# A planned attention and feed-forward kernel: a position table for the planner's rules, scaled down weights kept in memory, three more copy buffers

## The chip, the cores and the metric

The kernel runs on one core of a Trainium2 chip. The metric is device time in microseconds, as the median of several runs. Five engines work side by side, each through its own list of instructions: TensorE (PE, matrix products), VectorE (DVE), ScalarE (ACT), GpSimd (POOL) and SyncE (SP, which here only issues transfers).

## The reference

One transformer block over 2048 tokens of width 512, with 32 heads of 16, all in bf16. A condition vector c gives six vectors of shifts, scales and gates:

```
mod = silu(c) @ w_mod                     # sa, ca, ga, sb, cb, gb
h = layernorm(x) * (1 + ca) + sa
q, k, v = heads(h @ wqkv)                 # 32 heads of 16
o = softmax(q k^T / 4) v
x = x + ga * (o @ wo)
h = layernorm(x) * (1 + cb) + sb
x = x + gb * ((gelu(h @ w_gate) * (h @ w_up)) @ w_down)     # 512 -> 1792 -> 512
```

The score matrices have 32 x 2048 x 2048 elements, and each needs an exponential. That is what most of the time goes into.

## The kernel before

**Work.** The queries are cut into nine sets (`SETS`): seven of 256 tokens and two of 128. A unit is one set of queries with one group of four heads; the first two sets, and for the first heads the last two, are taken together. For each unit PE multiplies queries and keys 32 rows at a time into `ps_sc`, two halves of three banks of 512 columns (`qk`). An exponential turns a half into bf16 in `E`, and PE multiplies E with the values into `ps_pv` (`pv_mms`). At a unit's end (`unit_end`) DVE copies the sums to `osb`, a small transfer chain spreads the denominators, and DVE normalises into `onorm`.

**Two ways to an exponential.** One exponential instruction of ACT takes two or three banks. When it takes two, DVE turns the third into an exponential with integer arithmetic: a multiply and add on the scores gives the bits of a power of two (`bits` in `stream`, in the profile `dreg`, `kq`, `mreg<-ps_sc`). Four such banks make a quad, and each quad needs three shifted copies (`shift_task`, `128x2048 uint16`), which PE multiplies with scaled copies of the values (`vs`) to correct the error of the approximation. The quads' banks lie in buffers `kq`, the copies in buffers `sq`; `room` says which buffers a unit may take.

**Side work.** Everything else is put between the score products: projections, output projection (`side_wo`), second layernorm (`side_t2`) and the feed-forward layer (`side_ffn`), all through the bank `ps_mi`. The first six sets are the flow sets (`FLOW`): each set's feed-forward streams its gate, up and down weights from memory in pieces of 256 KB (`load`, `load_down`). Since the down weights are not scaled by gb, `down_fin` multiplies the sum by gb into `xw` and then adds it to the residual `xs`. For the last sets the weights stay (`weight_parts`), and `scale_down` multiplies the resident down weights by gb once on DVE.

**What sets the order.** The kernel's order is not written out by hand. `stream` runs a model of the engines while it records instructions: at each step it probes when an operation could start, and takes a score product, a value product, a piece of side work or a filler product. Its rules are constants: how far ahead a quad may be chosen (`AHEAD`, 96), how full DVE may be (700, 150), when a copy is urgent (`URGENT`, `LATE`), how much side work must be due (1536, one half of a piece), and `TUNE`, of which all sixteen rows are alike. What is recorded is a fixed list for each engine; at run time only semaphores hold an instruction back. Fillers are products whose result is not used; `short` asks for them when PE has worked too little in the last few microseconds.

**The head** (`prologue`) loads the first tokens and weights, computes the modulation columns (`mod_cols`) and the first layernorm, transposes and projects, with 512-column warm-up products (`warm_up`) between.

Instructions are recorded by helpers, so the profile's lines are those of the helpers: L328 matmul, L332 transpose, L341 activation, L345 tensor_tensor, L353 tensor_scalar, L358 scalar_tensor_tensor, L362 copy, L391 transfers.

## Time and profile before

| | |
|---|---|
| median of 3 runs | 818.45 us (818.15 to 819.36) |
| span of the profiled execution | 817.5 us |
| ACT busy | 783.2 us (96%) |
| PE busy | 750.5 us (92%) |
| DVE busy | 742.8 us (91%) |
| read from HBM, written | 50.04 MB, 2.35 MB |
| mean granted clock of TensorE | 1.00 |

The profiled execution is one run; what the profile tells of it is its span, from the first to the last instruction, 817.5 us. The timed runs are 0.65 to 1.9 us longer than that.

How to read the rows: a group has the line, the engine, the operation, what it writes and reads, the shape of both, how often it ran, its busy time together, the mean duration of one in ns, and how long its engine stood idle just before such instructions, with what ended most of that. Durations of neighbours on one engine overlap a little, so the distance from one start to the next is shorter than a duration. In the view by stretches each engine has its busy time in a stretch and, in brackets, its instructions.

### The profile page before, as it was taken

The numbers are of one execution on the slowest core, as the hardware profiler recorded it, in microseconds if no ns is written. First come the engines' busy times: TensorE is split into PE (matmuls) and PEld (weight loads), VectorE is DVE, ScalarE is ACT, GpSimd is POOL, SyncE is SP. The second block draws the span as 40 slices with busy tenths as digits, with TensorE's granted clock in tenths as the row PEclk, the third lists the DMA queues.
The fourth block names the chain that finished last, engine by engine and source line by source line (L and its number), as shares of the span: only waits on it lengthen the run. The fifth ranks groups of instructions, "written<-read, shape, count | busy, mean of one in ns | idle before, by whom it ended". The sixth has DMA issues, their size and how long they took to land.

```text
span 817.5 us, 37365 instructions
## 1 busy us (share of the span) xinstructions
PE 750.5 (92%) x17184; PEld 366.4 (45%) x17188; DVE 742.8 (91%) x1496; ACT 783.2 (96%) x746; POOL 4.6 (1%) x13
## 2 busy tenths in 40 slices
PE   7899999998999898989999899998998899888998
PEld 3333334343543454435443444444443444346567
DVE  6876898899999999999999999999999999989874
ACT  5999999999999999999999999999999999999962
POOL 2000000000000000000000000000000000000000
PEclk9999999999999999999999999999999999999999
DMA  9100000021530153104420442034233541200000
GB/s 292 63 6 20 10 9 10 10 71 40 168 112 16 52 155 93 35 21 134 122 63 16 136 121 61 16 105 133 63 106 88 165 126 36 67 10 10 19 13 14
DMA packets 94499, 57.38 MB, mean 70 GB/s; under 512 B 17029, under 2 KB 91910, under 8 KB 94342
## 3 DMA queue, kind: packets, MB, share of 16 engines
q1 hardware_dynamic: 93812, 54.47, 23.6%
q8 instruction: 134, 2.20, 1.2%
q10 hardware_dynamic: 530, 0.53, 0.2%
q14 instruction: 23, 0.19, 0.1%
HBM read 50.04 MB, written 2.35 MB: 64 GB/s over the span
## 4 chain that ended last, share of the span: by engine, by line
ACT 88%; PE 9%; DVE 1%; issue 0%; DMA 0%; SPq 0%; DVEq 0%
ACT E L341 85%; PE ps_sc L328 4%; PE ps_mi L328 3%; ACT wreg L341 3%; PE ps_pv L328 2%; DMA xs<-in_A_x_dram 0%; DVE osb L362 0%; DVE xs L345 0%; DVE dreg L353 0%; DVE st L381 0%; DVE wreg L353 0%; DVE nwt L345 0%; PE ps_sc L332 0%; DVE wreg L358 0%; DVE mreg L353 0%
## 5 line engine op out<-in xcount | busy, mean ns | idle before, releaser
L341 ACT ACTIVATE E<-ps_sc 128x1024 bf16<-128x1024 f32 (+2 forms) x700 | 758.7, 1319 | 19.1 <-PE ps_sc L328 19.0
L328 PE MATMUL ps_sc<-qT,kT 32*128 32x256 bf16 (+3 forms) x2048 | 202.2, 273 | 25.2 <-ACT E L341 21.1
L328 PE MATMUL ps_sc<-qo,kT 32*128 32x256 bf16 (+2 forms) x2048 | 202.2, 273 | 16.9 <-ACT E L341 15.5
L328 PE MATMUL ps_pv<-E,vaug 128*17 128x256 bf16 (+2 forms) x3204 | 154.1, 273 | 3.8 <-DVE osb L362 2.7
L353 DVE TENSOR_SCALAR dreg<-ps_sc 128x512 uint16<-128x512 f32 x200 | 135.5, 687 | 6.8 <-PE ps_sc L328 5.8
L328 PE MATMUL ps_mi<-wreg,mreg 128*32 128x256 bf16 x2816 | 116.6, 275 | 6.5 <-DVE wreg L362 3.4
L328 PEld LDWEIGHTS ps_sc<-qT,kT 32*128 32x128 bf16 (+1 forms) x2048 | 62.3, 92 | 117.3 <-ACT E L341 105.1
L328 PEld LDWEIGHTS ps_sc<-qo,kT 32*128 32x128 bf16 x2048 | 62.1, 92 | 105.6 <-ACT E L341 94.9
L328 PEld LDWEIGHTS ps_pv<-E,vaug 128*17 128x17 bf16 x3204 | 60.4, 89 | 59.6 <-issue 39.8
L328 PEld LDWEIGHTS ps_mi<-wreg,mreg 128*32 128x32 bf16 x2816 | 63.7, 96 | 42.8 <-issue 24.8
L328 PE MATMUL ps_pv<-mreg,vs 128*17 128x256 bf16 (+2 forms) x1840 | 80.9, 268 | 0.6 <-DVE mreg L353 0.3
L353 DVE TENSOR_SCALAR kq<-ps_sc 128x512 uint16<-128x512 f32 x104 | 70.9, 688 | 8.6 <-PE ps_sc L328 8.2
L353 DVE TENSOR_SCALAR mreg<-dreg 128x2048 uint16<-128x2048 uint16 x100 | 67.5, 682 | 2.2 <-PE ps_pv L328 2.2
L353 DVE TENSOR_SCALAR mreg<-ps_sc 128x512 uint16<-128x512 f32 x96 | 65.0, 688 | 4.5 <-PE ps_sc L328 4.3
L328 PEld LDWEIGHTS ps_pv<-mreg,vs 128*17 128x17 bf16 x1840 | 40.7, 91 | 15.1 <-issue 4.7
L353 DVE TENSOR_SCALAR mreg<-mreg 128x2048 uint16<-128x2048 uint16 x71 | 47.4, 686 | 0.0
L328 PE MATMUL ps_mi<-hreg,wreg 128*32 128x512 bf16 (+1 forms) x496 | 36.6, 376 | 0.4 <-DVE vaug L362 0.3
L362 DVE CAST wreg<-ps_mi 128x512 bf16<-128x512 f32 x49 | 33.6, 686 | 2.4 <-PE ps_mi L328 2.2
L345 DVE TENSOR_TENSOR wreg<-wreg 128x1024 bf16<-128x1024 bf16 (+1 forms) x56 | 34.5, 618 | 0.0
L353 DVE TENSOR_SCALAR sq<-dreg 128x2048 uint16<-128x2048 uint16 x49 | 33.7, 687 | 0.8 <-PE ps_pv L328 0.8
L358 DVE SCALAR_TENSOR_TENSOR wreg<-wreg,ps_mi 128x512 bf16<-128x512 bf16 x49 | 33.4, 682 | 1.0 <-ACT wreg L341 0.5
L353 DVE TENSOR_SCALAR mreg<-kq 128x2048 uint16<-128x2048 uint16 x48 | 32.5, 683 | 0.0
(193 smaller groups left out, 722.7 us busy)
## 6 DMA issues: line engine op xcount, KB each, us to landing
mreg<-in_B_w_up_dram SPq DMA_DIRECT2D x46, 256.0 KB, 3.2
mreg<-in_B_w_gate_dram SPq DMA_DIRECT2D x42, 256.0 KB, 3.3
dreg<-in_B_w_down_dram SPq DMA_DIRECT2D x18, 256.0 KB, 3.5
rb<-scr_rec SPq DMA_DIRECT2D x120, 32.0 KB, 2.0
mreg<-in_B_w_down_dram SPq DMA_DIRECT2D x12, 256.0 KB, 3.7
ereg<-in_B_w_down_dram SPq DMA_DIRECT2D x12, 256.0 KB, 3.8
mreg<-in_w_mod_dram SPq DMA_DIRECT2D x1, 2048.0 KB, 11.8
out_dram<-xs SPq DMA_DIRECT2D x15, 128.0 KB, 1.7
```

The costliest lines, as they stand in the source:

```text
L328: return self.rec("pe", lambda e: e.matmul(out, lhsT, rhs, start=start, stop=stop, tile_position=tp), [lhsT, rhs], [out], cost=(n, int(rhs ...
L341: return self.rec("act", lambda e: e.activation(out, in_, func, scale=scale, **kw), rd, wr, cost=self.cost("act", out, [in_], "act"))
L345: return self.rec(eng, lambda e: e.tensor_tensor(out, a, b, op), [a, b], [out], cost=self.cost(eng, out, [a, b], "tt"))
L353: return self.rec(eng, lambda e: e.tensor_scalar(out, a, s1, s2, **kw), rd, [out], cost=self.cost(eng, out, [a], "ts") + 60 * (len(rd) - 1 ...
L358: return self.rec("dve", lambda e: e.scalar_tensor_tensor(out, a, s, b, op0=op0, op1=op1), rd, [out], cost=self.cost("dve", out, [a, b], " ...
L362: return self.rec(eng, lambda e: e.tensor_copy(out, in_), [in_], [out], cost=self.cost(eng, out, [in_], "ts"))
```

## The change

1. The planner's constants become one row of fourteen numbers, and `TUNE` a table of 33 rows, one for each 64 positions of the score sequence (`rules`). In the order of a row: the ACT slack in which side work may start, the credit below which a quad may start in the later part, the number of waiting DVE steps, a DVE look-ahead, the two bounds on DVE's load, the old `LATE`, the old `URGENT`, how far ahead a quad may lie, the old `AHEAD`, the share of a piece that must be due, the credit at which side work goes first, the rate of credit in per cent, and DVE's lead in the background step.
2. The down weights are multiplied by gb in the first flow set, right after their load, and written to a new tensor `wd_scaled` in memory. All later loads read that tensor; `scale_down` and the second operation of `down_fin` go.
3. Three more buffers for shifted copies, in parts of `hreg`, `mreg` and `dreg` that are free in some stages; `room` opens them by stage. `ones` and `half`, which lay in that part of `dreg`, get tiles of their own. The loads of the last pieces of gate and down weights wait for the buffer in `hreg`.
4. In `prologue` six warm-up products go.
5. The model's least time of a product over the whole array is 158 columns instead of 64. This changes the planner's view only.

```diff
-AHEAD = (30, 44)
-URGENT = 9
-LATE = 2
-TUNE = ((600, 3500, 6, 120),) * 16
+STEP = 64
+RULES = (600, 3500, 6, 120, 700, 150, 2, 9, 96, 30, 2, 1536, 100, 150)
+TUNE = (
+    (1000, 4097, 6, 120, 700, 150, 2, 9, 96, 30, 2, 1536, 100, 150),
+    (600, 3500, 6, 120, 700, 150, 2, 3, 96, 30, 2, 1536, 100, 150),
+    (600, 3500, 6, 120, 700, 150, 2, 3, 96, 27, 3, 1536, 100, 0),
...
+)
-            end = t + max(cols + (12 if mode else 6), 64) / 2.4
+            end = t + max(cols + (12 if mode else 6), 64 if mode else 158) / 2.4
-        self.sq += [ereg[:, :], onorm[:, 2048:4096]]
+        self.sq += [ereg[:, :], onorm[:, 2048:4096], hreg[:, NFC * 256:NFC * 256 + 2048], mreg[:, 10240:12288], dreg[:, 10 * D:14 * D]]
-        self.ones = dreg[:, 10 * D:10 * D + P]
-        self.half = dreg[:, 10 * D + P:10 * D + 2 * P]
+        self.ones = sb("ones", [P, P], BF16)[:, :]
+        self.half = sb("half", [P, 2], BF16)[:, :]
+        self.wdg = self.dram("wd_scaled", [F, D], BF16).rearrange("(f p) n -> p f n", p=P)
-        self.warm_up(4)
+        self.warm_up(1)
         self.mod_cols(self.scp[:, 1, 0:8], 0, range(4))
-        self.warm_up(3)
-        dv = self.B_w_down.rearrange("(f p) n -> p f n", p=P)
+        dv = self.wdg
-        return ([piece(0, i, g[i]) for i in range(6)] + [piece(0, 6, g[6], [("ffn", 0)]), piece(2, 6, d[6], [("ffn", 0)])]
+        return ([piece(0, i, g[i]) for i in range(6)] + [piece(0, 6, g[6], [last, "sq"]), piece(2, 6, d[6], [last, "sq"])]
-    def scale_down(self):
...
-    def down_fin(self, bank, t, flow=False):
-        if flow:
-            self.tt("dve", self.xw, bank, self.gb[:, :], ALU.mult)
-        self.tt("dve", self.xs[:, t, :], self.xs[:, t, :], self.xw if flow else bank, ALU.add)
+    def down_fin(self, bank, t):
+        self.tt("dve", self.xs[:, t, :], self.xs[:, t, :], bank, ALU.add)
-                v = self.B_w_down.rearrange("(f p) n -> p f n", p=P)
-                self.task([("sp", lambda: self.dma("sp", self.wdst[i], v[:, 2 * i:2 * i + 2, :], "sd%d" % i))], ("wl", gi, 2, i))
+                v = self.wdg if gi else self.B_w_down.rearrange("(f p) n -> p f n", p=P)
+                steps = [("sp", lambda: self.dma("sp", self.wdst[i], v[:, 2 * i:2 * i + 2, :], "sd%d" % i))]
+                if not gi:
+                    steps += [lambda x=x: self.tt("dve", self.wdst[i][:, x, :], self.wdst[i][:, x, :], self.gb[:, :], ALU.mult) for x in range(2)]
+                    steps += [("sp", lambda: self.dma("sp", self.wdg[:, 2 * i:2 * i + 2, :], self.wdst[i], "ws%d" % i))]
+                self.task(steps, ("wl", gi, 2, i),
+                          (lambda: NSQ in self.sq_free) if i > 4 else (lambda: NSQ + 4 in self.sq_free) if i in (1, 2) else None)
-        return 0 if self.plain[tk[1][1]] * 512 <= URGENT * tk[1][1][3] else 2
+        return 0 if self.plain[tk[1][1]] * 512 <= self.tune[7] * tk[1][1][3] else 2
+    def rules(self, i):
+        self.tune = TUNE[min(i, len(TUNE) - 1)]
-                ok = range(NK if pool is self.quad_free else NSQ + (u in units[:4]))
+                ok = list(range(NSQ))
+                if ("ffn", FLOW - 1) in self.have:
+                    ok += [NSQ, NSQ + 3]
+                elif ("q", 3, NDC - 1) in self.have:
+                    ok += [NSQ + 2]
+                elif ("t2T", 0) not in self.have:
+                    ok += [NSQ, NSQ + 4]
-            self.tune = TUNE[min(pos // P, 15)]
+            if pos // STEP != stage:
+                stage = pos // STEP
+                self.rules(stage)
-                if len(mem) == CH and c > 2 and self.free["dve"] < max(t + 700, self.free["act"] + 150):
+                if len(mem) == CH and c > 2 and self.free["dve"] < max(t + self.tune[4], self.free["act"] + self.tune[5]):
-                    self.credit = min(self.credit + rate * len(items), 4096)
+                    self.credit = min(self.credit + rate * len(items) * self.tune[12] / 100, 4096)
```

The remaining lines of the diff put other numbers of the row in the place of the old constants in the same way.

## The prediction

> **What bounds the kernel now.** I read the page first (engines, chain), then busy time by stretch, then the groups of ScalarE and VectorE, last the timeline of the first 16 us.

> ```profile
> PE 750.5 (92%) x17184; PEld 366.4 (45%) x17188; DVE 742.8 (91%) x1496; ACT 783.2 (96%) x746; POOL 4.6 (1%) x13
> ...
> ACT 88%; PE 9%; DVE 1%; issue 0%; DMA 0%; SPq 0%; DVEq 0%
> ```

> ScalarE (ACT) is busy for 96% of the span, and 88% of the chain that ended last runs through it. VectorE (DVE) and TensorE (PE) come close, so the stretches must tell who waits. In the next view each row is a stretch, and each engine has its busy time in it.

> ```profile
> core 0: us, PE busy (x) PEld busy (x) DVE busy (x) ACT busy (x) POOL busy (x), PEclk, DMA share, GB/s
> 9.53:16.45 6.92, 4.89 (x72) 3.32 (x71) 3.84 (x12) 3.70 (x7) 0.00 (x0) 1.00 0.98 317
> 16.45:206.00 189.55, 174.64 (x3622) 71.83 (x3621) 162.81 (x355) 188.57 (x173) 0.31 (x1) 1.00 0.13 37
> 206.00:290.00 84.00, 77.78 (x1802) 37.74 (x1799) 81.95 (x156) 84.00 (x81) 0.00 (x0) 1.00 0.30 84
> 206.00:728.00 522.00, 483.59 (x11212) 232.62 (x11209) 502.52 (x957) 522.00 (x495) 0.00 (x0) 1.00 0.31 86
> 742.00:793.00 51.00, 46.19 (x1642) 30.35 (x1641) 42.30 (x96) 45.38 (x42) 0.00 (x0) 1.00 0.08 16
> 793.00:817.50 24.50, 21.23 (x280) 18.00 (x280) 11.23 (x31) 5.64 (x11) 0.00 (x0) 1.00 0.04 12
> ```

> From 16.45 to 206 us ACT is busy for 188.57 of 189.55 us, and from 206 to 728 us for all 522.00. DVE is busy there for 502.52, so it has 19.5 us left, 3.7%. In 742 to 793 us no engine is full (ACT 45.38 and PE 46.19 of 51), and from 793 us ACT hardly works. So in the long middle a change is worth what it takes off ACT, as long as DVE keeps up; in the head it is worth what it takes off the chain before the first exponential.

> ```profile
> L341 ACT ACTIVATE E<-ps_sc 128x1024 bf16<-128x1024 f32 x355 | 356.5, 1178 | 0.0
> L341 ACT ACTIVATE E<-ps_sc 128x1536 bf16<-128x1536 f32 x201 | 299.1, 1602 | 1.0 <-PE ps_sc L328 1.0
> ```

> In 126 to 741.5 us the exponentials waited 1.0 us in all, for scores of PE. Over the whole run:

> ```profile
> L341 ACT ACTIVATE E<-ps_sc 128x1024 bf16<-128x1024 f32 x432 | 434.9, 1169 | 2.0 <-PE ps_sc L328 2.0
> L341 ACT ACTIVATE E<-ps_sc 128x1536 bf16<-128x1536 f32 x260 | 385.9, 1591 | 3.8 <-PE ps_sc L328 3.8
> L341 ACT ACTIVATE wreg<-wreg 128x1024 bf16<-128x1024 bf16 x21 | 25.5, 1217 | 0.0
> ```
> ```profile
> L353 DVE TENSOR_SCALAR dreg<-ps_sc 128x512 uint16<-128x512 f32 x200 | 135.5, 687 | 6.8 <-PE ps_sc L328 5.8
> L353 DVE TENSOR_SCALAR kq<-ps_sc 128x512 uint16<-128x512 f32 x104 | 70.9, 688 | 8.6 <-PE ps_sc L328 8.2
> ```

> A group of 512 score columns goes either to ACT (two or three groups in one exponential) or, four at a time, to DVE, which builds the bits of the exponential (dreg, kq, mreg<-ps_sc) and then three shifted copies. One group costs ACT 1591-1169 = 422 ns: the two forms differ by 512 columns. The waits of dreg and kq for ps_sc, 6.8 and 8.6 us, are DVE standing before scores that PE had not finished.

> **The change, part by part.** The tables and buffers only steer a planner, so I counted the instructions of both programs as built.

> *More groups on DVE.* Exponentials: 432 of 1024 and 260 of 1536 columns before, 448 and 244 after. Their number stays at 692, and 16 groups leave ACT: 16 x 0.422 = 6.75 us less on the engine that bounds the middle. All 28 Tanh stay.

> On DVE these are 16 more bit builds and 12 more shifted copies. What one occupies is read from start to start, since the durations overlap:

> ```profile
> 403.14 0.68 DVE L353 TENSOR_SCALAR mreg<-mreg 128x2048 uint16<-128x2048 uint16 x1
> 403.73 0.69 DVE L362 CAST wreg<-ps_mi 128x512 bf16<-128x512 f32 x1
> 404.33 0.69 DVE L353 TENSOR_SCALAR sq<-kq 128x2048 uint16<-128x2048 uint16 x1
> 404.93 0.42 DVE L345 TENSOR_TENSOR wreg<-wreg 128x512 bf16<-128x512 bf16 x1
> 405.27 0.69 DVE L353 TENSOR_SCALAR mreg<-kq 128x2048 uint16<-128x2048 uint16 x1
> ```

> A read of 512 PSUM columns or a copy of 2048 takes 0.60 us, a 512-column product in SBUF 0.34. Added: 16 x 0.60 + 12 x 0.60 = 16.8 us.

> *Down weights scaled once.* For twelve row tiles the old finish multiplied the sum in PSUM by gb (12 x 0.60) and then added it (12 x 0.34); now one add reads PSUM (12 x 0.60). The last layers' 14 scalings (12 x 0.34 on xs, 2 on hreg) become 14 in the first pass. Net -12 x 0.34 = -4.1 us. So DVE has +16.8 - 4.1 = +12.7 us over the run. Counted with these prices between the ends of the attention units nearest to 206 and 728 us, 8.3 us of it fall into that stretch, from which ACT loses 2.9; the rest lies in the head and the tail, where DVE has more room (162.81 of 189.55 us, 42.30 of 51). There DVE then has 502.5 + 8.3 = 510.8 us in 519, 8.2 us idle instead of 19.5. It must follow with 98.4% busy. The nearest row, 206 to 290 us, has 81.95 of 84.00 (97.6%) and ACT still full. I therefore take +0.5 us of new ACT stalls; the ends are -2.7 (all that is idle on ACT before 742 us goes) and +11.3 (DVE's waits all stay, the rival below).

> *Stores.* Seven stores of 256 KB join SP's queue; the 42 loads stay, 35 of them now from the scaled copy. Each store waits on SP for two DVE scalings, and behind it in the queue stand the loads of the gate and up weights and the small transfers of the denominators. An issue takes SP about 0.5 us (1.81 in the views below), 3.5 us in all; SP is otherwise mostly waiting. I take 0 and bound it by -0.5 and +1: the cover is the matmuls of the layer, which wait for weights issued a chunk ahead. The later load of d6 and g6 has the same cover.

> *Three more buffers, rules by position.* They cost no instruction; their effect is in the counts. Filler matmuls drop from 172 to 112. PE has slack where they stand, 0.

> *Head.* Six of the 512-column warm-ups go (4 to 1, 3 to 0). ones and half move to tiles of their own, with as many memsets, off the chain.

> ```profile
> 1.25 2.31 PE L328 MATMUL ps_mi<-dreg 128*128 128x512 bf16 x5 [1.25 <-DVE dreg L369]
> ...
> 8.27 0.54 PE L328 MATMUL ps_sc<-sc_bf,mreg 128*128 128x1 bf16 x16 [0.33 <-DVE nwt L345]
> 8.67 1.02 PE L328 MATMUL ps_mi<-dreg 128*128 128x512 bf16 x4
> 9.53 0.54 PE L328 MATMUL ps_sc<-sc_bf,mreg 128*128 128x1 bf16 x16
> 10.15 0.59 PE L328 MATMUL ps_mi<-dreg 128*128 128x512 bf16 x2
> 10.58 0.72 PE L332 MATMUL ps_sc<-ident,dreg 128*128 128x128 bf16 x10
> ```
> ```profile
> 8.63 0.81 ACT L341 ACTIVATE dreg<-xs,nwt,rstd 128x512 bf16<-128x512 bf16 x1 [2.98 <-DVE nwt L358]
> ```
> ```profile
> 8.52 1.05 DVE L353 TENSOR_SCALAR dreg<-xs,mv,rstd 128x512 bf16<-128x512 bf16 x3
> 10.11 0.16 DVE L345 TENSOR_TENSOR modA<-modA,ps_sc 128x8 f32<-128x8 f32 x1 [0.54 <-PE ps_sc L328]
> 11.17 1.05 DVE L353 TENSOR_SCALAR hreg<-ps_sc,modA 128x256 bf16<-128x256 bf16 x3 [0.90 <-PE ps_sc L332]
> ```
> ```profile
> 1.81 0.47 SPq L391 DMA_DIRECT2D mreg<-in_w_mod_dram  x1
> ```
> ```profile
> mreg<-in_w_mod_dram SPq DMA_DIRECT2D x1, 512.0 KB, 7.0
> ```

> Columns of the first four: start, us, engine; of the last: the median us from issue to landing. The second batch of modulation columns (9.53) stands behind four warm-ups; behind one it can start at 8.67 + 0.22 = 8.89 (four take 9.53 - 8.67). Its weights, issued at 1.81, land 7.0 us later at 8.81, so that is allowed. It ends at 9.3. The transposes (10.58) then wait for the normed tiles, the second of which ACT finishes at 8.63 + 0.81 = 9.44. Eight transposes of the first half end near 9.7, and the modulation at 11.17 starts near 9.95. What is late next is that ACT norm. Gain 1.2 us; the low end is 0.6 (only the first step moves), the high end 1.3.

> *Tail.* After the last joint unit (columns 1792 to 2047, fourth head group) 90 groups were left for ACT, now 94, and one Tanh more; PE has 64 more 256-column matmuls of the last layers there.

> ```profile
> 745.38 0.71 PE L328 MATMUL ps_mi<-wreg,mreg 128*32 128x256 bf16 x17 [0.28 <-issue]
> ```

> 17 such matmuls take 0.71 us, with one latency, so at most 0.042 each: 64 x 0.042 = 2.7 us on PE, against 4 x 0.422 + 1.2 = 2.9 on ACT (a Tanh by its mean). I let them lie beside each other, since both engines have gaps there; the 16 groups above already count this end, as 20 groups and the Tanh are saved before that point.

> **The sum.** The profiled execution spans 817.5 us, 0.95 below the median of 818.45. 817.5 - 6.75 - 1.2 + 0.5 = 810.05; with the 0.95, 811.0 us.

> **Rivals.**
> *DVE becomes the bound (slower).* If all 19.5 us of DVE's idle time between 206 and 728 us are waits that cannot be filled (for scores, sums in ps_mi, ps_pv), the stretch needs 510.8 + 19.5 = 530.3 us instead of 519. ACT then stalls 11.3 us, because a bank that DVE has not read cannot take new scores: 811.0 - 0.5 + 11.3 = 821.8. It decides from 8 us of stall, that is when more than 16 of the 19.5 us remain. For it: DVE's waits for ps_sc are 6.8 and 8.6 us in only two groups. Against: in 206 to 290 us only 2 of 84 us were idle, so most of the waits were gaps without ready work, and the copy buffers give more ready work. Half of it (some 6 to 8 us) ends near no change.

> *The tail takes back part.* If in 742 to 793 us PE and ACT alternate instead of overlapping, PE's extra comes on top: 811.0 + 2.7 = 813.7. For it: between 742 and 793 us both have gaps of about 5 us, each waiting for the other. Against: 51 us hold the two with 4.8 to 5.6 us to spare.

> *The clock.* The five 512-column warm-ups of 1.25 us took 2.31, four at 8.67 only 1.02: TensorE starts at half rate. With six warm-ups fewer it could fall back; PE is busy for 4.89 us between 9.53 and 16.45, 4.3 without the two warm-ups at 10.15; at half rate that is at most 4.3 us more, 815.3. Against: no gap on PE in the new order of the head is longer than about 1 us.
> [...]

> **How the numbers follow.** The forecast (810 to 812) has 0.62; DVE as bound 0.16; half of that, no change, 0.05; the tail 0.11; the clock 0.06. This kernel's runs differ by 0.15%, so 0.2% (1.6 us) is what can be told. Faster: 0.62 + 0.11 + 0.06 = 0.79; same 0.05; slower 0.16. The range goes down to 807.8 (the stalls' low end, 811.0 - 0.5 - 2.7) and up to 818.5, which leaves out the slow rival. The likeliest case has 809 to 813.

> **What would show it.** Right: 448 and 244 exponentials with ACT full from about 15 to 732 us, its idle time there under 3 us; the first modulation of hreg near 9.95; DVE at 98% or more in the middle. Wrong: idle time of ACT before E in the middle beyond 4 us, with ps_sc from PE as releaser and DVE behind PE (the rival), the hreg modulation at 10.5 or later, or 512-column matmuls as slow after 9 us as the first five (the clock). I am also wrong if the joint unit's end comes 9 us earlier but the last exponential does not.

## The result and the profile after

The changed kernel took 814.43 us (median of 5 runs, 813.47 to 816.09), the kernel before beside it 819.36 (818.15 to 823.71): a ratio of 0.9936, interval 0.9919 to 0.9953. It is faster, but 3.4 us above the forecast of 811.0: inside the whole range (807.8 to 818.5), outside the 809 to 813 of the likeliest case. The profiled execution spans 811.7 us and took 813.47, so 1.8 us lie outside its span, where the forecast had 0.95.

First the page of the changed kernel: busy times, the granted clock in 40 slices, the chain that ended last, and what went through memory. Its lines are 33 further down than before (L341 is now L374, L328 is L361, L353 is L386).

```profile
PE 751.3 (93%) x17217; PEld 367.2 (45%) x17217; DVE 749.9 (92%) x1512; ACT 777.2 (96%) x746; POOL 4.9 (1%) x13
...
PEclk8799999999999999999999999999999999999999
...
HBM read 50.04 MB, written 4.18 MB: 67 GB/s over the span
...
ACT 72%; PE 14%; DVE 11%; DMA 2%; issue 1%; SPq 0%; DVEq 0%
```

ACT lost 6.0 us, DVE gained 7.1. The seven stores are there (4.18 MB written instead of 2.35). New are the 8 and the 7 in the first two slices of the clock, up to about 40 us. The page of the kernel before has nines alone:

```profile
PEclk9999999999999999999999999999999999999999
```

Less of the chain runs through ACT (72% instead of 88%), more through DVE and PE, and a little through loads of gate and up weights. The next view shows ACT as full as before in the middle, so this chain is one of several of nearly the same length there. The same stretches as in the prediction:

```profile
core 0: us, PE busy (x) PEld busy (x) DVE busy (x) ACT busy (x) POOL busy (x), PEclk, DMA share, GB/s
9.53:16.45 6.92, 4.86 (x76) 3.01 (x80) 4.93 (x15) 4.72 (x9) 0.00 (x0) 0.89 1.10 339
16.45:206.00 189.55, 178.31 (x3584) 71.89 (x3576) 165.13 (x359) 186.37 (x174) 0.56 (x1) 0.97 0.11 31
206.00:728.00 522.00, 486.03 (x11360) 235.56 (x11361) 511.17 (x971) 521.90 (x498) 0.00 (x0) 1.00 0.33 91
742.00:793.00 51.00, 47.24 (x1530) 32.29 (x1525) 41.95 (x104) 42.45 (x42) 0.00 (x0) 1.00 0.07 16
```

From 206 to 728 us DVE is busy for 511.17 us (forecast 510.8), and ACT still fills 521.90 of 522. From 16.45 to 206 us ACT has 3.2 us idle instead of 1.0, at a mean clock of 0.97. The exponentials of the whole run by form, and from 126 to 728 us:

```profile
L374 ACT ACTIVATE E<-ps_sc 128x1024 bf16<-128x1024 f32 x448 | 449.5, 1164 | 2.7 <-PE ps_sc L361 2.4
L374 ACT ACTIVATE E<-ps_sc 128x1536 bf16<-128x1536 f32 x244 | 363.6, 1591 | 4.5 <-PE ps_sc L361 4.5
```
```profile
L374 ACT ACTIVATE E<-ps_sc 128x1024 bf16<-128x1024 f32 x364 | 365.4, 1173 | 0.1
L374 ACT ACTIVATE E<-ps_sc 128x1536 bf16<-128x1536 f32 x185 | 277.8, 1613 | 0.0
```

So the waits are not in the middle (0.1 us in 600). ACT's timeline of the head has them:

```profile
10.06 0.56 ACT L374 ACTIVATE hreg<-ps_sc,modA 128x256 bf16<-128x256 bf16 x1 [0.49 <-PE ps_sc L365]
13.17 1.45 ACT L374 ACTIVATE E<-ps_sc 128x1536 bf16<-128x1536 f32 x1 [0.58 <-PE ps_sc L361]
15.46 2.37 ACT L374 ACTIVATE E<-ps_sc 128x1024 bf16<-128x1024 f32 x2 [0.84 <-PE ps_sc L361]
18.25 1.02 ACT L374 ACTIVATE E<-ps_sc 128x1024 bf16<-128x1024 f32 x1 [0.42 <-PE ps_sc L361]
19.67 2.36 ACT L374 ACTIVATE E<-ps_sc 128x1536 bf16<-128x1536 f32 x2 [0.40 <-PE ps_sc L361]
23.23 3.71 ACT L374 ACTIVATE E<-ps_sc 128x1536 bf16<-128x1536 f32 x3 [1.20 <-PE ps_sc L361]
27.33 1.02 ACT L374 ACTIVATE E<-ps_sc 128x1024 bf16<-128x1024 f32 x1 [0.39 <-PE ps_sc L361]
28.81 1.45 ACT L374 ACTIVATE E<-ps_sc 128x1536 bf16<-128x1536 f32 x1 [0.46 <-PE ps_sc L361]
```

The first modulation of hreg starts at 10.01 us on DVE, beside ACT's at 10.06 (forecast 9.95), and the first exponential at 13.17 instead of 14.33: the 1.2 us of the head. Then ACT waits for scores six times up to 29 us, 3.7 us in all; the kernel before lost 0.7 us there. The next view cuts the head where the granted clock changes:

```profile
8.12:11.54 3.42, 2.77 (x41) 2.14 (x41) 3.07 (x13) 2.29 (x4) 0.00 (x0) 1.00 1.14 312
11.54:14.95 3.41, 1.66 (x29) 0.86 (x28) 1.76 (x6) 2.22 (x3) 0.00 (x0) 1.00 1.10 339
14.95:18.36 3.41, 3.26 (x71) 1.75 (x70) 2.03 (x6) 2.48 (x3) 0.00 (x0) 0.50 1.08 357
18.36:21.78 3.42, 3.31 (x25) 0.71 (x25) 3.14 (x13) 3.02 (x3) 0.00 (x0) 0.50 1.03 411
21.78:25.19 3.41, 3.41 (x24) 1.10 (x20) 1.49 (x7) 2.21 (x3) 0.00 (x0) 0.50 0.44 155
25.19:28.61 3.42, 3.42 (x36) 0.95 (x33) 2.65 (x14) 2.77 (x3) 0.00 (x0) 0.50 0.02 5
28.61:32.02 3.41, 3.22 (x46) 1.37 (x43) 2.91 (x9) 3.21 (x3) 0.00 (x0) 1.00 0.00 0
```

TensorE runs at half rate from 14.95 to 28.61 us, four stretches of 3.41 us. In the profiled execution before it ran at full rate from 7.17 us on. This is the rival "the clock", to which the prediction gave 0.06.

The span went down by 5.8 us: 1.16 to the first exponential, 4.52 from there to the table load behind the last exponential, 0.10 after it. The 4.52 are made up so: ACT is busy for 5.86 us less (764.06 for 769.92; the forecast for the columns was 6.75), it waits 3.04 us more before 29 us, and 1.70 less after that.

### The profile page after: what moved, and what is told of

It is laid out like the page before. It is cut to its first block, busy times and chain, and to the rows that moved or that the text cites. A ratio compares the mean times of both kernels' runs of the same rounds, so it can differ in the third digit from the quotient of the medians.

```text
span 811.7 us, 37453 instructions
## 1 busy us (share of the span) xinstructions
PE 751.3 (93%) x17217; PEld 367.2 (45%) x17217; DVE 749.9 (92%) x1512; ACT 777.2 (96%) x746; POOL 4.9 (1%) x13
## 3 DMA queue, kind: packets, MB, share of 16 engines
HBM read 50.04 MB, written 4.18 MB: 67 GB/s over the span
## 4 chain that ended last, share of the span: by engine, by line
ACT 72%; PE 14%; DVE 11%; DMA 2%; issue 1%; SPq 0%; DVEq 0%
ACT E L374 70%; PE ps_sc L361 6%; PE ps_mi L361 5%; PE ps_pv L361 3%; ACT wreg L374 2%; DVE dreg L386 2%; DVE mreg L386 2%; DVE wreg L395 1%; DVE wreg L378 1%; DVE kq L386 1%; DMA mreg<-in_B_w_up_dram 1%; DVE wreg L391 1%; DMA mreg<-in_B_w_gate_dram 1%; DVE wreg L386 0%; DMA xs<-in_A_x_dram 0%
## 5 line engine op out<-in xcount | busy, mean ns | idle before, releaser
L374 ACT ACTIVATE E<-ps_sc 128x1024 bf16<-128x1024 f32 (+2 forms) x700 | 751.6, 1306 | 20.5 <-PE ps_sc L361 20.2
L361 PE MATMUL ps_sc<-qT,kT 32*128 32x256 bf16 (+3 forms) x2048 | 200.0, 274 | 20.9 <-ACT E L374 17.5
L361 PE MATMUL ps_sc<-qo,kT 32*128 32x256 bf16 (+2 forms) x2048 | 197.7, 274 | 17.1 <-ACT E L374 14.7
L361 PE MATMUL ps_pv<-E,vaug 128*17 128x256 bf16 (+2 forms) x3168 | 152.8, 274 | 0.7 <-DVE vaug L395 0.3
L386 DVE TENSOR_SCALAR dreg<-ps_sc 128x512 uint16<-128x512 f32 x208 | 140.3, 683 | 6.4 <-PE ps_sc L361 5.5
L361 PE MATMUL ps_mi<-wreg,mreg 128*32 128x256 bf16 x2816 | 112.0, 275 | 6.5 <-DVE wreg L391 2.2
L361 PEld LDWEIGHTS ps_sc<-qT,kT 32*128 32x128 bf16 (+1 forms) x2048 | 60.4, 92 | 110.4 <-ACT E L374 93.0
L361 PEld LDWEIGHTS ps_sc<-qo,kT 32*128 32x128 bf16 x2048 | 60.2, 92 | 108.5 <-ACT E L374 94.7
L361 PEld LDWEIGHTS ps_pv<-E,vaug 128*17 128x17 bf16 x3168 | 60.2, 89 | 58.0 <-issue 38.7
L361 PEld LDWEIGHTS ps_mi<-wreg,mreg 128*32 128x32 bf16 x2816 | 64.9, 96 | 39.6 <-issue 22.6
L386 DVE TENSOR_SCALAR kq<-ps_sc 128x512 uint16<-128x512 f32 x108 | 72.8, 682 | 5.1 <-PE ps_sc L361 5.0
L386 DVE TENSOR_SCALAR mreg<-ps_sc 128x512 uint16<-128x512 f32 x100 | 67.2, 683 | 2.4 <-PE ps_sc L361 2.1
L361 PE MATMUL ps_pv<-mreg,vs 128*17 128x256 bf16 (+2 forms) x1552 | 67.0, 267 | 2.5 <-issue 1.4
L386 DVE TENSOR_SCALAR mreg<-dreg 128x2048 uint16<-128x2048 uint16 x93 | 62.2, 678 | 0.0
L361 PEld LDWEIGHTS ps_pv<-mreg,vs 128*17 128x17 bf16 x1552 | 33.7, 91 | 14.9 <-issue 5.4
L361 PE MATMUL ps_mi<-hreg,wreg 128*32 128x512 bf16 (+1 forms) x496 | 37.8, 381 | 0.7 <-DVE qT L386 0.6
L391 DVE SCALAR_TENSOR_TENSOR wreg<-wreg,ps_mi 128x512 bf16<-128x512 bf16 x49 | 33.2, 678 | 0.9 <-PE ps_mi L361 0.7
L386 DVE TENSOR_SCALAR mreg<-mreg 128x2048 uint16<-128x2048 uint16 x49 | 32.7, 681 | 0.0
L395 DVE COPY osb<-ps_pv 128x256 f32<-128x256 f32 (+2 forms) x63 | 25.9, 411 | 4.9 <-PE ps_pv L361 4.6
L374 ACT ACTIVATE wreg<-wreg 128x1024 bf16<-128x1024 bf16 (+1 forms) x28 | 30.2, 1080 | 0.0
```

Of the source, the lines that this page charges most:

```text
L361: return self.rec("pe", lambda e: e.matmul(out, lhsT, rhs, start=start, stop=stop, tile_position=tp), [lhsT, rhs], [out], cost=(n, int(rhs ...
L374: return self.rec("act", lambda e: e.activation(out, in_, func, scale=scale, **kw), rd, wr, cost=self.cost("act", out, [in_], "act"))
L386: return self.rec(eng, lambda e: e.tensor_scalar(out, a, s1, s2, **kw), rd, [out], cost=self.cost(eng, out, [a], "ts") + 60 * (len(rd) - 1 ...
L391: return self.rec("dve", lambda e: e.scalar_tensor_tensor(out, a, s, b, op0=op0, op1=op1), rd, [out], cost=self.cost("dve", out, [a, b], " ...
L395: return self.rec(eng, lambda e: e.tensor_copy(out, in_), [in_], [out], cost=self.cost(eng, out, [in_], "ts"))
```

## Experiments

All experiments compute the whole reference. The kernel before ran beside them: 818.95 us beside the first four, 819.85 beside the next four, 819.66 beside the last four. These are three different chips, so the ratios compare better than the medians. In the table, the profiled execution's span is cut at the first exponential and at the table load behind the last one; "half rate" counts stretches of 3.41 us at half clock from 8 us to 800 us.

| run | median us | ratio to before | span | first exponential | to the table load | rest | half rate |
|---|---|---|---|---|---|---|---|
| before | 818.45 | | 817.5 | 14.33 | 775.19 | 28.0 | 0 |
| the change | 814.43 | 0.9936 [0.9919, 0.9953] | 811.7 | 13.17 | 770.67 | 27.9 | 4 |
| 1 the change again | 813.21 | 0.9939 [0.9918, 0.9961] | 814.5 | 14.12 | 771.89 | 28.5 | 5 |
| 2 warm-ups back | 815.43 | 0.9953 [0.9939, 0.9967] | 815.4 | 13.18 | 773.83 | 28.4 | 6 |
| 3 fillers off the chain | 811.56 | 0.9907 [0.9891, 0.9923] | 809.2 | 13.29 | 768.22 | 27.7 | 0 |
| 4 before, fewer warm-ups | 820.89 | 1.0028 [1.0008, 1.0048] | 819.3 | 15.03 | 775.24 | 29.0 | 4 |
| 5 before, new head, fillers | 819.74 | 0.9999 [0.9983, 1.0015] | 816.9 | 15.18 | 772.89 | 28.8 | 1 |
| 6 run 3, raw down weights | 813.93 | 0.9932 [0.9909, 0.9954] | 811.8 | 13.02 | 772.64 | 26.2 | 0 |
| 7 run 3, no copy buffers | 825.64 | 1.0056 [1.0027, 1.0086] | 826.9 | 13.18 | 782.71 | 31.0 | 5 |
| 8 run 3, one rule set | 818.94 | 0.9993 [0.9979, 1.0007] | 816.7 | 12.84 | 777.74 | 26.1 | 1 |
| 9 run 3, thin places filled | 812.25 | 0.9911 [0.9885, 0.9938] | 807.0 | 12.86 | 766.53 | 27.6 | 0 |
| 10 runs 2 and 3 together | 814.14 | 0.9932 [0.9905, 0.9959] | 814.3 | 13.32 | 773.29 | 27.7 | 4 |
| 11 run 3, 16 groups twice | 822.87 | 1.0044 [1.0025, 1.0062] | 821.1 | 12.99 | 780.68 | 27.5 | 3 |
| 12 runs 9 and 10 together | 812.09 | 0.9913 [0.9891, 0.9935] | 808.0 | 12.88 | 767.34 | 27.8 | 0 |

### Is it the missing warm-ups? Runs 1 to 4

Run 1 is the changed kernel as it stands.

> The changed kernel again, as the yardstick for the three beside it. Granted clock 0.99 as in its first runs, ratio to the kernel before about 0.993. If the half clock between 15 and 29 us came by chance, the clock is 1.00 and the ratio 0.990.

Run 2 puts the warm-ups back in their places:

```diff
-        self.warm_up(1)
+        self.warm_up(4)
         self.mod_cols(self.scp[:, 1, 0:8], 0, range(4))
+        self.warm_up(3)
```

> The changed kernel with the seven warm-ups of before in their places (4 and 3). Theory (the missing warm-ups let TensorE fall to half clock): clock 1.00, first exponential at 14.3 us instead of 13.2, ACT idle between the first exponential and 30 us under 1 us instead of 3.7: 1.2 lost, 3.0 won, so some 1.8 us faster than the changed kernel. Rival (the table's other order and its fewer fillers cause it): half clock as before the restoration, 1.2 us slower than the changed kernel.

Run 3 leaves them out and puts the same product where PE otherwise waits: two ahead of the copies of qT in `prologue`, four behind the first key product in `prologue_rest`.

```diff
+        self.warm_up(2)
         for h in range(2):
             self.act(self.qT[:, 0, 256 * h:256 * h + 256], qb[h], ACT.Copy, scale=Q_SCALE)
...
             self.mm(self.pv[:, 256:512], self.wqkv[:, dc, 512:512 + P], self.hT[:, dc, 256:512], start=(dc == 0), stop=(dc == NDC - 1))
+        self.warm_up(4)
```

> The changed kernel with six 512-column warm-ups in two places of the head where TensorE stands idle anyway (two before the first copies of q, four after the second half's key product). Theory of the clock: clock 1.00 and first exponential still near 13.2 us (at most 0.3 later), so about 3 us faster than the changed kernel, span near 808.7. Rival (the order causes it): half clock stays, time equal to the changed kernel or up to 0.5 us slower.

Run 4 takes the warm-ups out of the kernel before:

```diff
-        self.warm_up(4)
+        self.warm_up(1)
         self.mod_cols(self.scp[:, 1, 0:8], 0, range(4))
-        self.warm_up(3)
```

> The kernel before with the six warm-ups taken out and nothing else; the split between ACT and DVE stays 432 and 260. Theory of the clock: first exponential 1.2 us earlier, clock below 1.00 and about 3 us of ACT idle before 30 us: some 2 us slower than the kernel before. Rival: clock 1.00 and 1.2 us faster.

Runs 1 to 3 have the same lists of instructions for ACT and DVE as the change. Run 4 differs from the kernel before in more than the warm-ups: the planner starts from another head, so ACT's list is the same only for 43 instructions (up to 49 us) and DVE's for 54 (up to 22 us). The first falls of run 4 can be compared with the kernel before, its middle can't.

Run 2 fell at half rate at the same place as the change itself, warm-ups or not; run 3 did not fall. Two stretches each: run 2, then run 3.

```profile
11.58:14.99 3.41, 1.66 (x29) 0.86 (x27) 1.76 (x6) 2.22 (x3) 0.00 (x0) 1.00 1.10 339
14.99:18.40 3.41, 3.19 (x71) 1.74 (x66) 2.07 (x6) 2.54 (x3) 0.00 (x0) 0.50 1.09 360
```
```profile
11.23:14.65 3.42, 3.29 (x47) 1.78 (x45) 1.78 (x6) 2.56 (x4) 0.00 (x0) 1.00 1.10 340
14.65:18.06 3.41, 2.56 (x81) 1.30 (x78) 3.09 (x11) 2.74 (x4) 0.00 (x0) 1.00 1.09 356
```

In the stretch ahead of the fall PE has little to do (1.66 us, as in the change); with the fillers it has 3.29. So my first theory, the missing warm-ups alone, falls for this place. Run 2's median, 2.2 us above run 1's, is nearer to the rival's 1.2 us than to the gain of 1.8 that the theory forecast. The theory holds for another place: run 1 fell from 11.02 us on, after this stretch, in which the removed warm-ups used to stand,

```profile
7.61:11.02 3.41, 2.25 (x37) 1.78 (x38) 2.99 (x14) 1.89 (x4) 0.00 (x0) 1.00 1.18 296
11.02:14.44 3.42, 2.86 (x25) 1.49 (x26) 0.98 (x3) 1.48 (x4) 0.00 (x0) 0.50 1.10 341
```

and run 4 at 10.04. Run 4 is slower than the kernel before by 0.28%, and its first exponential came at 15.03 us, later and not 1.2 us earlier: without its fillers that step of the change gained nothing. How much of the 0.28% is the other plan stays open.

| streamed of 3.41 us | stretches | followed by half rate |
|---|---|---|
| under 1.40 us | 23 | 22 |
| 1.40 to 1.50 | 11 | 3 |
| 1.50 to 1.70 | 48 | 1 |
| over 1.70 | 3190 | 0 |

At half rate the same columns take twice the time (0.427 us for 512, against 0.216). Ten half-rate stretches with 1.9 to 2.9 us streamed were followed by another, 23 with 2.6 to 3.2 us by full rate. The four of the change had 2.68, 2.89, 2.65 and 2.95 us, and full rate came behind the fourth.

The 1.4 us were read from the traces of both kernels and of runs 1 to 8, and stand in the expectations of run 9. In the four traces after that, all six full-rate stretches under 1.40 us were followed by half rate, of the others one (1.43 us, in run 11).

In the thin stretch of the change the longest wait of PE was 1.2 us, and the clock fell: that gaps stay near 1 us, as the prediction argued, was not enough. What separates the stretches of these runs is the streamed share: 1.40 of 3.41 us, about 41%.

With this one can look for thin places in a trace: starting points, at full rate, whose next 3.41 us hold less than 1.40 us. Where the grid of a run hit one, a fall came 22 times of 23.
- Before: 12.42 to 13.65 us, where PE waits for qT, and 1.9 us of starting points behind 20 us (363, 759). The grid of the profiled run lay at 10.58 and 14.00, so it missed the first.
- The change: 5.36 to 7.63, where the warm-ups were, and from 11.26 on, again at the waits for qT. The grid at 4.71, 8.12 and 11.54 missed the first and hit the second.
- Run 1: the grid at 7.61 hit the first (from 5.10 on). Run 2 has only the second (from 11.26 on), hit at 11.58. Run 3 has only the first (5.00 to 7.75), and its grid at 7.82 just missed it. Behind 20 us its plan, which is the change's, has 3.3 us (84, 319, 619, 754).

The second place, in PE's timeline of the change, with its two waits:

```profile
12.73 0.39 PE L361 MATMUL ps_sc<-qT,kT 16*128 16x512 bf16 x3 [0.56 <-ACT qT L374]
13.06 0.62 PE L361 MATMUL ps_pv<-hreg,wreg 128*32 128x256 bf16 x16
14.86 0.98 PE L361 MATMUL ps_sc<-qT,kT 16*128 16x512 bf16 x5 [1.19 <-DVE qT L386]
```

So the change made the first place, and in the middle its plan, as run 3 shows it, has 3.3 us of thin starting points instead of 1.9. That the fillers that went are the reason is likely, but no run puts just them back. The second place is about as wide in both (1.2 us before; 1.0, 11.38 to 12.39, in run 3 with its six fillers left out of the count); that the profiled execution before missed it and that of the change hit it was the offset of the grid. What differs there is how long a fall lasts: four, four and two stretches in the change and runs 1 and 2, one stretch each time in runs 4 and 5, which have the plan of before up to some 20 us (three falls up to 17 us). Of the 23 executions of before beside runs 1 to 4 none has a mean clock under 0.994, of the 17 of the change eight have. Why a fall lasts longer in the plan of the change was not tried by itself and stays open.

### What is the new head worth with the clock held? Run 5

The kernel before with run 4's edit and run 3's.

> The kernel before with the changed kernel's head (4 warm-ups to 1, 3 to 0) and with the six small products that kept the clock in the third experiment (two ahead of the qT copies, four after the first key product). No group of scores moves: 432 and 260 exponentials. Theory (the head saves 1.2 us, and the fourth experiment lost it only because the clock fell): the first exponential stands near 13.2 us, the clock holds 1.00 until after 29 us, and the time is 1.2 us below the kernel before, 817.7 where that is at 818.9. Rival one (the head's gain is worth nothing further down, because something else sets the middle): no difference. Rival two (the clock falls for another reason than idle places on PE): half rate again within 10 to 29 us and 0.5 us or more slower than before, as the fourth experiment's 820.9.

No difference (0.9999), and the clock did fall: its grid at 7.65 us hit the first thin place (from 5.00 on in its trace), and the first exponential came at 15.18. So the removed warm-ups did double duty: without them the clock fell here from 11.06 us on, as in runs 1 and 4 (from 11.02 and 10.04). The first theory's 1.2 us did not come, rival two's half-rate stretch did, though without its loss of time. ACT's list is that of run 4, and DVE's nearly so: with the six fillers this plan is level with the kernel before, without them 0.28% slower, though the intervals overlap.

### Which part moves the groups? Runs 6 to 8

All three stand on run 3. Run 6 loads raw down weights and scales as before (with `scale_down` back and no `ws` stores):

```diff
-                v = self.wdg if gi else self.B_w_down.rearrange("(f p) n -> p f n", p=P)
+                v = self.B_w_down.rearrange("(f p) n -> p f n", p=P)
...
-    def down_fin(self, bank, t):
-        self.tt("dve", self.xs[:, t, :], self.xs[:, t, :], bank, ALU.add)
+    def down_fin(self, bank, t, flow=False):
+        if flow:
+            self.tt("dve", self.xw, bank, self.gb[:, :], ALU.mult)
+        self.tt("dve", self.xs[:, t, :], self.xs[:, t, :], self.xw if flow else bank, ALU.add)
```

Run 7 closes the new buffers:

```diff
-                ok = (3, 4) if pool is self.quad_free else (3, 4, 5, 8)
+                ok = (3, 4) if pool is self.quad_free else (3, 4, 5)
...
-                if ("ffn", FLOW - 1) in self.have:
-                    ok += [NSQ, NSQ + 3]
...
+                if u in units[:4]:
+                    ok += [NSQ]
```

Run 8 has one rule set:

```diff
-TUNE = (
-    (1000, 4097, 6, 120, 700, 150, 2, 9, 96, 30, 2, 1536, 100, 150),
...
+TUNE = (RULES,) * 33
```

> The third experiment's kernel (811.6 us, 448 and 244 exponentials) with the scaled down weights undone: raw loads, the two-step finish for the twelve tiles, and 14 scalings in the tail. As built the rules then move 4 groups to VectorE instead of 16 (436 and 256). Theory (the middle is ScalarE's columns, 0.422 us each): 12 groups come back, 12 x 0.422 = 5.1 us, so 816.6. Rival (the scaling's 4.1 us of VectorE work is itself what the change gained, the groups only follow): VectorE has the 12 groups' 12.6 us less and 4.1 us more, the time stays within 1.5 us of 811.6.

> The third experiment's kernel without the three additional copy buffers; rules by position and scaled weights stay. As built no group moves then (432 and 260). Theory (ScalarE's columns): all 16 groups come back, 6.75 us, 811.6 + 6.75 = 818.3, with VectorE at 91% or less. Rival (the rules by position have their own worth, beside the groups): below 817.

> The third experiment's kernel with one rule set for all positions in place of the table; buffers and scaled weights stay. As built 4 groups move instead of 16 (436 and 256). Theory (ScalarE's columns): 12 x 0.422 = 5.1 us back, 816.6, and VectorE near 8 us less busy between 206 and 728 us than the changed kernel's 511.2. Rival (the table also sets fillers and the order around the tail, and without it PE's waits come on top): 818 or more. Rival two (the table costs as much as it gains): within 1.5 us of 811.6.

As built 4, 0 and 4 groups move to DVE instead of 16, so each part is needed for the count. The times missed the forecasts on both sides. Run 6 lost 2.6 us of span against run 3, not 5.1: 4.4 up to the table load, but 1.6 less behind it and 0.3 less ahead. Runs 7 and 8 lost more than the columns, as these rows of the exponentials of run 3, run 7 and run 8 show by their idle time:

```profile
L374 ACT ACTIVATE E<-ps_sc 128x1024 bf16<-128x1024 f32 x448 | 450.5, 1171 | 3.1 <-PE ps_sc L361 3.0
```
```profile
L374 ACT ACTIVATE E<-ps_sc 128x1024 bf16<-128x1024 f32 x432 | 433.4, 1152 | 9.2 <-PE ps_sc L361 8.9
```
```profile
L340 ACT ACTIVATE E<-ps_sc 128x1024 bf16<-128x1024 f32 x436 | 436.1, 1155 | 8.7 <-PE ps_sc L327 8.7
```

Some 6 us of new waits for scores in either. In run 7 about half of the waits of the middle lie in half-rate stretches (416, 634 us), and what follows the table load takes 3.3 us longer; in run 8 they are two waits at 135 and 149 us (1.9 and 2.0) at full rate and one at 234 us (1.8) in a half-rate stretch. The rules by position without the buffers are slower than the kernel before, the buffers without the rules the same as it.

### Filling the thin places: runs 9, 10 and 12

Run 9 adds to run 3 one filler product ahead of the scores of eight exponentials. `unplanned` records it and sets the planner's model back, so that all other instructions stay in their order:

```diff
+THIN = (66, 67, 68, 280, 553, 554, 555, 672)
...
+                if c in THIN:
+                    self.unplanned(lambda: self.mm(self.scp[:, s0, :], *filler))
                 self.qk([(seq[m], k) for m, k in items])
```

> The third experiment's kernel (811.6 us) with one additional filler product of 512 columns ahead of the scores of eight exponentials (numbers 66, 67, 68, 280, 553, 554, 555, 672), which the planner doesn't count, so every other instruction stays in its order. Theory (the clock is set in fixed stretches of 3.41 us: one in which PE streams for less than about 1.4 us is followed by one at half rate, and where the grid lies differs from run to run): the third experiment's trace has places near 84, 319, 619 and 754 us where a stretch of 3.41 us holds less than 1.4 us, together 3.3 us of starting points, so one half-rate stretch per run on average, about 1 us each. Filled, no half-rate stretch stands between 30 and 780 us, every run's mean clock is 0.996 or more, and the median is 810.6. Rival (the half-rate stretches in the middle fall by chance or by load over a longer time): half-rate stretches at these places as before, and the fillers cost up to 8 x 0.2 = 1.6 us: 811.6 to 813.2.

Run 10 is run 3 with the warm-ups of run 2, run 12 is run 10 with run 9's fillers.

> The third experiment's kernel with the warm-ups of the kernel before back as well (1 to 4, 0 to 3), so that both thin places of the head are filled: the one from 5 to 11 us (the removed warm-ups) and the one from 11.3 to 16 us (PE's waits for qT). Theory (fixed stretches): the clock holds 1.00 up to 80 us in the profiled run, and a first exponential at 13.2 if the first release comes before 5 us, at about 14.3 if it comes near 7 us, since the first warm-ups then run at half rate longer and the restored ones stand in the chain. So the head's 1.2 us is lost in part of the runs: 811.6 to 812.4. Rival (the warm-ups cost the chain 1.2 us always): first exponential at 14.3 whatever the release, 812.8.

> The ninth and the tenth experiment together: warm-ups back, both head fillers, and the fillers at the thin places of the middle. Theory (fixed stretches): no half-rate stretch ahead of 780 us in any phase of the grid, every run's mean clock 0.997 or more, runs closer together than in the third experiment (810.4 to 813.9 there), median 810.6 to 811.5. Rival (the clock falls by chance): clocks of single runs down to 0.994 as before, and 811.6 to 813.

Run 10 fell at just the places that run 3's trace had named: starting points at 84, 319 and 619 us there, and stretches from 84.62, 320.14 and 623.93 us here. The first two rows are run 10, the other two are run 9 in the same stretches, with its fillers:

```profile
84.62:88.03 3.41, 2.87 (x57) 1.43 (x53) 3.38 (x9) 3.41 (x4) 0.00 (x0) 1.00 0.00 0
88.03:91.45 3.42, 3.42 (x30) 0.69 (x26) 2.54 (x7) 3.31 (x3) 0.00 (x0) 0.50 0.00 0
```
```profile
84.62:88.03 3.41, 3.40 (x65) 1.66 (x65) 3.38 (x9) 3.41 (x3) 0.00 (x0) 1.00 0.00 0
88.03:91.45 3.42, 3.30 (x49) 0.94 (x41) 2.64 (x7) 3.42 (x4) 0.00 (x0) 1.00 0.00 0
```

The first stretch has 2.87 us of busy PE in run 10, but only 1.27 of streaming; in run 9 it has 1.64.

The profiled executions of runs 9 and 12 kept 1.00 to 800 us, and run 9 holds the shortest span of all (807.0 us; that execution took 808.75). But the medians missed: 812.25 for 810.6, and 812.09, just above 810.6 to 811.5. Both lie where the rivals put them, and so do the clocks of single runs. Run 10's 814.14 lies above its theory and its rival. The reason lies in the other executions, for which only the mean clock is known: three of six in run 9 and four of six in run 12 had 0.999 or 1.000 (808.75 to 812.37 us), the others 0.994 to 0.996 (814.06 to 815.94). A stretch at half rate takes 0.002 off the mean clock (half of 3.41 in some 810 us; the four of the change give its 0.992), so these fell two or three times, at places that the profiled execution does not show as thin. Where these fell stays open, also why they lost 4 to 5 us for it: the thin places of one trace do not tell those of every execution. So the fillers of the middle are not shown to be worth anything in the median; run 3, with the ratio 0.9907, beats both kernels.

On the head's price run 10 does not decide between my two cases. Its first exponential came at 13.32 us with the first release of the clock at 6.11; in run 12 it came at 12.88 (release at 4.96), in run 2 at 13.18 (4.75). Without the warm-ups, where the clock did not fall ahead of it, it stands at 12.84 to 13.29 (the change and runs 3, 6 to 9 and 11). So no price of the warm-ups shows in these three, beside a spread of 0.45 us.

### The price of ScalarE's columns: run 11

```diff
+TWICE = range(120, 600, 30)
...
+                if c in TWICE:
+                    self.unplanned(lambda: self.act(self.E[:, e0:e0 + 1, :], self.scp[:, s0:s0 + 1, :], ACT.Exp, scale=EXP_SCALE))
                 self.act(self.E[:, e0:e0 + n, :], self.scp[:, s0:s0 + n, :], ACT.Exp, scale=EXP_SCALE)
```

> The third experiment's kernel with 16 groups of 512 columns put through ScalarE a second time (every 30th exponential from the 120th to the 570th, same input and output, result unchanged), which the planner doesn't count: all other instructions stay in their order. It measures the price of ScalarE's columns in the middle by itself. One such instruction should occupy 0.06 + 0.42 = 0.48 us (0.904 us from start to start for 1024 columns is two of 0.422 and 0.06), so 7.7 us of ScalarE. Theory (ScalarE is the bound from 126 to 728 us, every column there counts in full): 811.6 + 7.7 = 819.3. Rival (VectorE or PE bound it as well since VectorE is at 98%, so ScalarE's columns count in part, as the sixth experiment's 12 groups gave 2.6 us of 5.1 between the profiled spans): 815.5 or less.

The one execution at a clock of 1.000 took 819.97 us, those of run 3 810.43 and 810.95: 9.0 to 9.5 us more, for a forecast of 7.7. (The median, 822.87, holds half-rate stretches in most executions.) The doubled instructions took longer than I had reckoned:

```profile
L384 ACT ACTIVATE E<-ps_sc 128x512 bf16<-128x512 f32 x16 | 12.4, 777 | 0.0
```

In the timeline it is 0.87 us on average from the start of one to the start of the next exponential, not 0.48. The last 0.09 of it is a wait, whose cause was not tried. Not all of that is lost: in the profiled execution, from 91 to 586 us at full rate, 13 doubled ones put the exponentials 8.2 us further behind those of run 3, 0.63 each. So the run does not give the price of 512 columns by itself. It does show that time on ScalarE in the middle counts in full, and the rival (815.5 or less) falls: none of the nine executions is under 819.85.

## Why the prediction was right, and where it was not

1. **More groups on DVE: right.** 448 and 244, and 16 x 0.422 = 6.75 us. With the clock held (run 3) the part from the first exponential to the table load is 775.19 - 768.22 = 6.97 us shorter: ACT is busy for 6.6 us less and waits 0.4 less. Run 11 shows that ACT's time counts in full there.
2. **DVE keeps up: right.** 511.17 us for 510.8. The +0.5 of new stalls was not needed there: the exponentials waited 0.1 us in 600. "DVE becomes the bound", with 0.16, did not come. Two figures on the way were wrong and changed nothing: over the whole run the sum had +12.7 us for DVE, and the page shows +7.1 (742.8 to 749.9); and the 6.8 and 8.6 us before dreg and kq are all of their idle time, of which the rows put 5.8 and 8.2 down to scores.
3. **Down weights and stores: nothing speaks against 0.** ACT's exponentials waited 0.1 us in the middle, whatever ended it. Run 6 doesn't isolate them, since its plan differs elsewhere too.
4. **Head, a gain of 1.2 us: right in this execution, not shown as a price.** The step said the modulation columns stand behind the warm-ups. In the profiled execution before (first release at 7.17 us) the first exponential came at 14.33, in the change at 13.17. With the warm-ups back it came at 12.88 to 13.32, with releases from 4.75 to 6.11, no later than without them. One profile of before showed one offset of the grid, and I priced it as the kernel's; that the late release is what made the warm-ups cost 1.2 us there fits, but was not tried by itself.
5. **Fillers, "PE has slack where they stand, 0": the step that failed.** The products that went cost no PE time, but the warm-ups kept the stretch from 5 to 11 us above 1.40 us streamed: runs 1, 4 and 5 fell there, runs 2, 10 and 12 did not. For the 60 fillers of the middle the same is likely, not shown. Against the clock rival I argued that no gap of PE was longer than about 1 us (it was 1.2). That the longest gap decides was my assumption, which no run shows; the runs put the streamed share of a stretch in its place. That rival had 0.06 and should have had most of the chance, at a smaller price than the 4.3 us that it carried: 3.0 us of new waits in the profiled execution. With them ACT's idle time from 15 to 732 us was 4.1 us, so that sign of being right (under 3) failed; in run 3 it was 1.3. That this one execution fell at the waits for qT is chance, since the kernel before has that place too; the executions together show the change. Over its 12 executions in run 1 the change spans 809.7 to 811.5 us where the mean clock was 0.998 and 816.7 to 818.8 where it was 0.985 to 0.987. None of its 17 executions reached 1.000; of the kernel before, 5 of the 23 beside runs 1 to 4 did.
6. **Tail: right.** From the table load to the end 27.9 us for 28.0, and from 741.5 us to the table load ACT waited 2.5 us for 3.6, so the rival of the tail did not come. But "their effect is in the counts", said of the rules, holds for this plan only: over the plans of runs 6 to 8 this part goes from 26.1 to 31.0 us, and waits for scores differ by 6 us, at nearly equal counts.

With the clock held the sum nearly stands: run 3 spans 809.2 us and took 811.56 in the median, for a forecast of 810.05 and 811.0. The second agreement is part luck. The sum's 0.95 us between span and median was too small, since every timed execution whose span is listed took at least 1.68 us longer than it, and the span came out 0.85 shorter than forecast. Luck, too, is that run 3's grid missed the thin place that it left open, from 5 to 8 us: two of its five executions kept a clock of 1.000. Of the 3.4 us that the change missed the forecast by in the first measurement, and 2.2 in run 1, run 3 gets back 1.65 against run 1 on the same chip (813.21 to 811.56), where the two intervals just overlap. Against the kernel before beside them, the forecast was 7.45 us less; measured were 4.93, 5.74 in run 1 and 7.39 in run 3.

## What to carry to other kernels

- Before products that "only fill" are removed, work out for each place how long PE streams in any 3.41 us, not how long its longest wait is. Here 22 of 23 full-rate stretches under 1.40 us were followed by half rate for at least the next 3.41 us, and the busy head of the change stayed there for 13.65.
- A product that keeps the clock belongs where PE waits for another engine: at the waits for qT the six off the chain did for the clock what six on the chain did not (PE busy for 3.29 of 3.41 us there in run 3, which stayed at full rate, and for 1.66 in run 2, which fell).
- A cost read in the head of one profiled execution can belong to that execution's offset of the clock's grid: here 1.2 us, with the release at 7.17 us, which did not show with releases from 4.75 to 6.11. Look at a second one before pricing it.

## What the runs showed of the hardware that was not expected

- TensorE fell to half rate in the middle of a full kernel, with no wait of PE in the stretch ahead of a fall longer than 1.6 us (run 2, ahead of 758.74 us), mostly under 1.2, and PE's busy time in the stretch at 1.7 to 3.0 us of 3.41. One such stretch (84.62 to 88.03 us in run 10) was busy for 2.87 us and waited for 0.5 in all, but 32 of its 57 products had one column: 1.1 us of busy time, in a stretch with 1.27 us streamed.
- The half-rate stretches that were followed by full rate had 2.6 to 3.2 us streamed of 3.41, about twice the 1.40 us that parted the stretches at full rate, where the same columns take half the time. Those between 2.6 and 2.9 went either way.
- The same instructions gave a first exponential at 13.17 and at 14.12 us in two executions of the changed kernel, with half rate from 14.95 and from 11.02 us on.
